# A fused attention, Fourier-mix and FFN kernel: a fourth 8 KB buffer, five FFN tiles resident, other transfer numbers in the list schedule

## The chip, the cores and the metric

The kernel runs on one core of one Trainium2 chip. The metric is device time in microseconds (us), the median of several executions. TensorE is PE, its weight loads PEld, VectorE DVE, ScalarE ACT, GpSimd POOL, and SyncE (SP) issues most of the DMAs.

## The reference, cut to what matters

```python
def reference(q, k, v, w_ch1, w_ch2):        # B=8, H=8, S=576, D=64
    s = where(mask[h], q @ k.T / 8, -1e9)    # window 32; heads 4..7: every 4th of 128
    x = softmax(s) @ v                       # -> x: (8, 576, 512)
    u = x + real(fft(fft(x, axis=1), axis=2))
    un = (u - mean(u)) / sqrt(var(u) + 1e-6) # over the 512 channels
    return u + relu(un @ w_ch1) @ w_ch2      # 512 -> 2048 -> 512
```

The two weights arrive as 64-bit floats; the kernel turns their bits into 32-bit floats itself.

## The kernel before, in words

There are three kinds of work.

**Attention** (lines 475 to 589) runs batch by batch. For a pair of heads it loads `kb`, `tq` and `vt`, multiplies scores (`sc`, line 507), masks and takes the maximum on DVE (`pm`, `mx`, line 515), exponentiates on ACT (line 521), transposes on PE (line 534), multiplies by the values (`av`, line 541), divides on DVE (`xt`, line 553, 96 of these in all) and stores to DRAM (line 588).

**The mix** (`mix`, lines 642 to 818) of a batch loads the stored rows as `x` and `xt` (lines 660 and 669), folds them on POOL and DVE, multiplies by cosine and sine tables (lines 723 and 769), adds on DVE (lines 783 and 785) and POOL, normalises, and stores `us`.

**The FFN** treats the 2048 hidden columns as 16 tiles of 128. A weight tile has a half of `w_ch1` and a half of `w_ch2`. Preparing a half (`prep`, from line 822) takes a 512 KB load (line 842), four DVE instructions (lines 845, 848, 851 and 854), two on ACT (lines 843 and 856) and a POOL subtraction (line 857). Every product is three matmuls, since each operand is held as a high and a low part.

- *Resident tiles*, `NF1` of them (`wa1`, `wa2`, 8 KB a partition for a tile), are prepared at the start, staged through the `ut` buffers. With them the first `NE[c]` tiles of a chunk of 512 tokens are worked off early, while attention and mix still run: `fill` does this for 256 tokens at a time (up: 128x256 matmuls at line 871, `h` at lines 877 and 879; down: line 887) and stores the sums as `part` (lines 907 and 908).
- *Late tiles* take memory that becomes free. When the attention is done, `first()` opens space for `NFA` = 4 tiles (from tile `NF1` on) and a pool with two stage buffers `wst`. When all of the mix and all of the early FFN work is done (but not the stores of its sums), `second()` opens `wbb` for the rest. The DMAs of a half wait for these gates; half one of a tile behind the second gate is staged in `ut`, half two in `wst`.
- The *late stage* goes chunk by chunk, nine chunks. A step is an up of 512 tokens into a bank `ff` (12 matmuls, line 871), relu on ACT and the low part on DVE into a buffer `hh` (lines 877 and 879), and a down (12 matmuls, line 887). `up` of step f+1 stands ahead of `down` of step f. At a chunk's end `finish` adds the parts and stores the output.

The buffers `ut` (`utb`, line 408, `NUT` of them, 8 KB a partition each) serve all of these in turn, in the order in which the program asked for them: staged weight halves, transposed tokens for `fill`, tokens of a late chunk, and the rows in `finish`.

**What sets the order.** Each operation is entered into `Plan` with an engine, a cost, what it reads and writes, and a priority. `Plan.run` (from line 243) is a list scheduler: it goes through its own modelled time, starts on each engine the ready operation of best priority for which a buffer is free, and writes the operations out in that order. Each engine then works strictly in that order. A DMA takes, in that model, its turn in one pipe and then a time to land (lines 317 and 318); SP has at most eight under way.

Of the kernel before, what the change touches and what calls it, by code (L numbers as in the profile page):

```python
# [10 lines left out]
F32R = mybir.dt.float32r  # L11
# [8 lines left out]
P = 128  # L20
KT = C // P
NF = FF // P
NF1 = 6
NE = (6, 6, 6, 6, 5, 5, 4, 4, 0)
TOK = 4 * P
TOK1 = 2 * P
NX = 4
NKB = 3
NV = 4
NTQ = 2  # L30
NUT = 3
NUC = 2
NH = 6
NLATE = 4
# [143 lines left out]
class Plan:  # L178
# [56 lines left out]
    def run(self):  # L235
        ops = self.ops
        busy = {}
        avail, soon = {}, {}
        turn = {t: 0 for t in self.tags}
        events = [0.0]  # L240
        dma = 0.0
        for o in ops:
            busy.setdefault(o.eng, 0.0)
            avail.setdefault(o.eng, [])
            soon.setdefault(o.eng, [])
            if not o.waits:
                heapq.heappush(soon[o.eng], (o.ready, o.num))
                heapq.heappush(events, o.ready)
        order = []
        used, clock = {}, [0, False]  # L250
        lanes = {e: [] for e in busy}

        def place(o, now):
            need = []
            if o.nbytes and len(lanes[o.eng]) >= 8 and lanes[o.eng][-8] > now:
                return False
            for b in o.bufs:
                if b.tag is None or b.ap is not None or b.free_at is not None:
                    continue
                line, k = self.tags[b.tag], turn[b.tag]  # L260
                if line[k] is not b:
                    return False
                if k >= self.slots[b.tag]:
                    old = line[k - self.slots[b.tag]]
                    if old.left or old.free_at > now:
                        return False
                need.append(b)
            for b in need:
                turn[b.tag] += 1
                b.free_at = -1.0  # L270
            return True

        while events:
            now = heapq.heappop(events)
            while events and events[0] <= now:
                heapq.heappop(events)
            again = True
            while again:
                again = False
                for eng in busy:  # L280
                    if busy[eng] > now:
                        continue
                    while soon[eng] and soon[eng][0][0] <= now:
                        _, n = heapq.heappop(soon[eng])
                        heapq.heappush(avail[eng], (ops[n].prio, n))
                    held, got = [], None
                    while avail[eng]:
                        e = heapq.heappop(avail[eng])
                        if place(ops[e[1]], now):
                            got = ops[e[1]]  # L290
                            break
                        held.append(e)
                        if len(held) > 60:
                            break
                    for e in held:
                        heapq.heappush(avail[eng], e)
                    if got is None:
                        continue
                    again = True
                    got.start = now  # L300
                    order.append(got)
                    cost = got.cost
                    if eng == "PE":
                        win = int(now / WINDOW)
                        while clock[0] < win:
                            load = used.get(clock[0], 0.0) / WINDOW
                            clock[1] = load > 0.45 if clock[1] else load > 0.75
                            clock[0] += 1
                        cost *= 1 if clock[1] else 2
                        used[win] = used.get(win, 0.0) + min(cost, (win + 1) * WINDOW - now)  # L310
                        used[win + 1] = used.get(win + 1, 0.0) + max(0.0, now + cost - (win + 1) * WINDOW)
                    end = now + cost
                    busy[eng] = end
                    heapq.heappush(events, end)
                    done = end
                    if got.nbytes:
                        dma = max(dma, end + 0.65) + got.nbytes / 3.6e5
                        done = dma + 1.0
                        lanes[eng].append(done)
                        heapq.heappush(events, done)  # L320
                    for a in got.after:
                        lag = self.OWN[eng] if a.eng == eng else self.LAG[eng]
                        a.ready = max(a.ready, done + lag)
                        a.waits -= 1
                        if not a.waits:
                            heapq.heappush(soon[a.eng], (a.ready, a.num))
                            heapq.heappush(events, a.ready)
                    for b in got.bufs:
                        b.left -= 1
                        b.free_at = max(b.free_at or 0.0, done + self.LAG[eng])  # L330
                        if not b.left:
                            heapq.heappush(events, b.free_at)
        if len(order) != len(ops):
            left = [o for o in ops if o.start is None]
            raise RuntimeError(f"{len(left)} operations can't be placed: {[(o.eng, o.num, o.prio) for o in left[:5]]}")
        self.length = max(busy.values())
        for o in order:
            o.fn()
# [29 lines left out]
def fused_kernel(ctx: ExitStack, tc, q, k, v, w1, w2, seq, tail, chn, alt, mask, ident, perm, flip, out):  # L368
    nc = tc.nc
    plan = Plan()  # L370
# [12 lines left out]
    pools = {}  # L383
# [18 lines left out]
    def ffnb(tag, shape, dtype=F32, bufs=2):  # L402
        return plan.buf(lambda: pools["ffn"], tag, shape, dtype, bufs)

    def fixed(pool_, shape, dtype, name):
        return Buf(ap=pool_.tile(shape, dtype, name=name))

    def utb(i=0):
        return ffnb("ut", [P, 2, KT, TOK1], F32R, NUT)

    flip_sb = fixed(const, [P, 8], I32, "flip_sb")
    wa1 = [fixed(const, [P, 2, KT, P], F32R, f"wa1_{f}") for f in range(NF1)]
    wa2 = [fixed(const, [P, 2, C], F32R, f"wa2_{f}") for f in range(NF1)]
    mask_sb = fixed(heads, [QB, 3, KB], F32, "mask_sb")
# [446 lines left out]
    def prep_w(f, d1, d2, stage, gate, prio):  # L861
        prep(w1.rearrange("(j k) f -> j k f", k=KT)[:, :, P * f:P * f + P], True, d1, stage(0), gate, prio)
        prep(w2[P * f:P * f + P], False, d2, stage(1), gate, prio)
# [148 lines left out]
    def early(c):  # L1012

        return NE[c]

# [19 lines left out]
    n_att = len(plan.ops)  # L1035
    for f in range(NF1):
        prep_w(f, wa1[f], wa2[f], utb, (), P_W + P_WF * f)
# [5 lines left out]
    n_side = len(plan.ops)  # L1043
    split = NF1 + NFA

    def weights(pool_, fs):
        for f in fs:
            wb1[f].ap = pool_.tile([P, 2, KT, P], F32R, name=f"wb1_{f}")
            wb2[f].ap = pool_.tile([P, 2, C], F32R, name=f"wb2_{f}")

    def first():
        att_ctx.close()
        weights(ctx.enter_context(tc.tile_pool(name="wba", bufs=1, side="right")), range(NF1, split))
        pools["stage"] = stage_ctx.enter_context(tc.tile_pool(name="stage", bufs=1, side="right"))
# [10 lines left out]
    def switch(fn, gate, after):  # L1065
        sw = add("NONE", 0.0, fn, (), gate, 0)
        for o in after:
            o.after.append(sw)
            sw.waits += 1

    wb1, wb2 = [[Buf() for f in range(NF)] for i in range(2)]
    gate1, gate2, gate3 = Buf(ap=0), Buf(ap=0), Buf(ap=0)
    switch(first, [gate1] + wb1[NF1:split] + wb2[NF1:split], plan.ops[:n_att])
    switch(second, [gate2] + wb1[split:] + wb2[split:], [o for o in plan.ops[:n_side] if o not in apart])
# [20 lines left out]
    for c in range(NCH):  # L1095
        where, gate = (("wbb", gate2), ("late", gate3))[c % 2]
        ut = load_ut(c, gate, where, LAST + c) if c else ut0
        accs = [bank(t) for t in spare[c % 3]]
        first = early(c)
        for f in range(first, NF):  # L1100
            w = (wb1 if f >= NF1 else wa1)[f]
            h = plan.buf(lambda: pools["wbb"], "hh", [P, 2, TOK], F32R, 3)
            h = up(ut, w, bank("ff"), h, LAST + c + f / NF, cut=True)
            if pend is not None:
                lower(*pend)
            pend = (c, f, h, accs, first, LAST + c + f / NF + 0.1)
# [24 lines left out]
```

## Time and profile before

| | us |
|---|---|
| median of 3 runs | 1156.83 |
| lowest, highest | 1151.93, 1158.43 |
| the profiled execution's own time | 1156.17 |
| its span | 1154.4 |
| PE busy, DVE busy | 1096.1, 595.6 |
| mean granted TensorE clock | 0.985 |

The profiled execution has 1.77 us outside its span and lies 0.66 us below the median. A row of the windows view gives, for a stretch of the span, the busy time of each engine with the number of instructions, the granted clock, the busy share of the DMA engines and their rate. In a row of instruction groups stand line, engine, operation, output <- input, shapes, count, then busy time and the mean duration of one in ns, then the engine's idle time just before and what ended it. Durations of matmuls overlap: the time of one is read from the distance of two starts.

### The profile page before, as it was taken

To read this page: it belongs to the slowest core of one execution; us is meant where nothing else is said; L and a number is where in the kernel's file an instruction comes from. 1 tells how busy PE (TensorE), PEld (TensorE's weight loads), DVE (VectorE), ACT (ScalarE), POOL (GpSimd) and SP (SyncE) were. 2 spreads that over 40 slices of the span, in tenths; PEclk is the share of its full clock that TensorE was granted. 3 is DMA by queue.
4 is the path that set the end of the run, shared out by engine and by line. 5 is a ranking of instruction groups with operands and counts; after the bars stand their busy time and mean duration, and the time that the engine had idled before them with its cause. 6 is when DMAs were issued, how large, how long until landed. Compare 5 with 4: busy or idle time off the path is not lost.

```text
span 1154.4 us, 17385 instructions
## 1 busy us (share of the span) xinstructions
PE 1096.1 (95%) x6112; PEld 920.5 (80%) x6112; DVE 595.6 (52%) x1949; ACT 417.1 (36%) x987; POOL 290.6 (25%) x346
## 2 busy tenths in 40 slices
PE   5878989999999998999998999999999999999998
PEld 4667878887888887889866888888888888888886
DVE  5899887666667657873387414141314141312111
ACT  4876656546455543433243212121212121121210
POOL 1245464233242315540045112020202020020100
PEclk9999999999999999999999999999999999999999
DMA  9985475455374426433354504050505040310201
GB/s 289 261 264 155 130 215 163 143 145 165 103 199 133 126 60 185 132 115 92 83 192 110 146 19 128 19 140 7 146 1 145 2 128 19 104 43 18 74 1 36
DMA packets 100966, 133.71 MB, mean 116 GB/s; under 512 B 9400, under 2 KB 60024, under 8 KB 100880
## 3 DMA queue, kind: packets, MB, share of 16 engines
q1 hardware_dynamic: 97296, 123.71, 37.5%
q0 software_dynamic: 3040, 8.09, 2.6%
q8 instruction: 48, 0.79, 0.3%
q10 hardware_dynamic: 544, 0.82, 0.2%
q14 instruction: 38, 0.31, 0.1%
HBM read 95.82 MB, written 36.75 MB: 115 GB/s over the span
## 4 chain that ended last, share of the span: by engine, by line
PE 73%; DVE 13%; DMA 6%; issue 2%; ACT 2%; POOL 1%; SPq 1%; DVEq 0%; ACTq 0%; POOLq 0%
PE ff L871 27%; PE sc L887 9%; PE mix L887 8%; PE ff L887 6%; PE sc L507 4%; PE pt L887 4%; PE av L887 4%; PE av L541 3%; PE mix L723 2%; PE mix L769 2%; DVE pm L515 2%; DMA x<-xsm 1%; PE pt L534 1%; DMA us<-uc 1%; DMA ut<-in_w_dram 1%
## 5 line engine op out<-in xcount | busy, mean ns | idle before, releaser
L879 DVE SCALAR_TENSOR_TENSOR hh<-ff,hh 128x512 fp32r<-128x512 f32 x102 | 70.1, 688 | 338.5 <-ACT hh L877 329.1
L877 ACT ACTIVATE hh<-ff 128x512 fp32r<-128x512 f32 x102 | 60.8, 596 | 328.5 <-PE ff L871 328.4
L871 PE MATMUL ff<-utwbb,wb 128*128 128x512 f32 x600 | 148.4, 397 | 2.1 <-ACT utwbb L995 1.2
L521 ACT ACTIVATE pm<-pm,mx 96x128 f32<-96x128 f32 x384 | 130.4, 394 | 54.8 <-DVE mx L515 51.8
L871 PEld LDWEIGHTS ff<-utwbb,wb 128*128 128x128 f32 x600 | 113.7, 190 | 29.3 <-POOL utwbb L998 2.5
L871 PE MATMUL ff<-ut,wa 128*128 128x256 f32 x816 | 115.1, 292 | 7.7 <-ACT row L907 4.7
L931 POOL DMA_INDIRECT ut<-us,flip_sb x20 | 19.4, 969 | 385.3 <-DMA out_dram<-ut 291.3
L871 PE MATMUL ff<-utlate,wb 128*128 128x512 f32 x480 | 116.1, 391 | 0.0
L507 PE MATMUL sc<-kb,tq 128*96 128x256 f32 x384 | 107.1, 399 | 8.9 <-DMA kb<-in_k_dram 7.6
L871 PEld LDWEIGHTS ff<-ut,wa 128*128 128x128 f32 x816 | 104.1, 193 | 10.7 <-ACT row L907 5.3
L871 PEld LDWEIGHTS ff<-utlate,wb 128*128 128x128 f32 x480 | 90.1, 188 | 19.8
L541 PEld LDWEIGHTS av<-vt,ptsb 128*96 128x96 f32 x768 | 79.8, 170 | 29.7 <-issue 12.5
L515 DVE CUSTOM_DVE_ANT_0 pm<-sc,mask_sb 96x128 f32<-96x128 f32 x384 | 92.0, 279 | 21.8 <-PE sc L507 17.2
L887 PE MATMUL ff<-wa,h 128*128 128x512 f32 x408 | 101.2, 398 | 0.4 <-DVE h L879 0.4
L541 PE MATMUL av<-vt,ptsb 128*96 128x65 f32 x768 | 84.6, 253 | 16.6 <-DVE xt L553 14.8
L887 PE MATMUL sc<-wb,hh 128*128 128x512 f32 x360 | 93.1, 393 | 5.1 <-DVE hh L879 5.1
L887 PE MATMUL mix<-wb,hh 128*128 128x512 f32 x360 | 92.1, 391 | 0.0
L887 PEld LDWEIGHTS ff<-wa,h 128*128 128x128 f32 x408 | 75.2, 189 | 16.8 <-DVE h L879 0.6
L887 PEld LDWEIGHTS sc<-wb,hh 128*128 128x128 f32 x360 | 67.3, 188 | 21.2 <-DVE hh L879 6.6
L978 DVE STREAM_TRANSPOSE ut<-ut 128x512 f32<-128x512 f32 (+1 forms) x68 | 66.6, 1020 | 31.5 <-DMA ut<-us 29.9
L887 PEld LDWEIGHTS mix<-wb,hh 128*128 128x128 f32 x360 | 67.6, 188 | 14.8
L507 PEld LDWEIGHTS sc<-kb,tq 128*96 128x96 f32 x384 | 56.9, 170 | 22.3 <-DVE kb L450 7.6
(147 smaller groups left out, 1676.2 us busy)
## 6 DMA issues: line engine op xcount, KB each, us to landing
vt<-in_v_dram SPq DMA_DIRECT2D x32, 390.0 KB
us<-uc SPq DMA_DIRECT2D x36, 257.0 KB
tq<-in_q_dram SPq DMA_DIRECT2D x32, 288.0 KB
ut<-in_w_dram SPq DMA_DIRECT2D x18, 512.0 KB
ut<-us SPq DMA_DIRECT2D x36, 256.0 KB
kb<-in_k_dram SPq DMA_DIRECT2D x62, 144.0 KB
part<-row SPq DMA_DIRECT2D x32, 256.0 KB
ut<-part SPq DMA_DIRECT2D x32, 256.0 KB
```

Of the source, the lines that this page charges most:

```text
L507: nc.tensor.matmul(sc()[:QB, 256 * n:256 * n + 256], lhsT=tq()[:, cols], rhs=kb()[:, :, keys], start=True, stop=True,)
L515: nc.vector.tensor_tensor_reduce(pm()[:, i], sc()[:QB, KB * i:KB * i + KB], mask_sb()[:, masks[blocks[i // 2]]], -0.125, 3.0e38, ALU.add, ...
L521: add("ACT", 0.295, lambda i=i: nc.scalar.activation(out=pm()[:, i], in_=pm()[:, i], func=AF.Exp, bias=mx()[:, i:i + 1], scale=-1.0), ((mx ...
L541: add("PE", 0.16, lambda i=i: nc.tensor.matmul(av()[:QB, 65 * i:65 * i + 65], lhsT=pt()[:, i], rhs=vt()[:, i % 2, blocks[i // 2]], start=T ...
L723: nc.tensor.matmul(ps()[:, :NSP], lhsT=lt, rhs=tab, start=(m == 0 and n == 0), stop=(m == 2 and n == count - 1),)
L769: nc.tensor.matmul(ps()[:n, :NEP], lhsT=ys[i]()[:, dt, a, rows], rhs=chn_sb[i]()[:, dt, c], start=(dt == 0 and x == 0), stop=(i == 1 and d ...
L871: nc.tensor.matmul(z()[:, :n_tok], lhsT=wf()[:, a, kk], rhs=ut()[:, p, kk], start=(kk == 0 and n == 0), stop=(kk == KT - 1 and n == 2),)
L877: add("ACT", act(n_tok) - 0.05, lambda: nc.scalar.activation(out=h()[:, 0, :n_tok], in_=z()[:, :n_tok], func=AF.Relu), (z,), ((h, 0),), prio)
L879: add("DVE", dve(n_tok), lambda: nc.vector.scalar_tensor_tensor(h()[:, 1, :n_tok], z()[:, :n_tok], 0.0, h()[:, 0, :n_tok].bitcast(F32), op ...
L887: nc.tensor.matmul(acc(), lhsT=h()[:, a, P * s:P * s + P], rhs=wf()[:, p], start=(first and n == 0), stop=(last and n == 2),)
L931: add("POOL", 1.04, lambda: nc.gpsimd.indirect_dma_start(u(), None, us[idx // 4](), bass.IndirectOffsetOnAxis(ap=flip_sb()[:, 4 * kk + idx ...
L978: nc.vector.transpose(out=o[back], in_=x[:, g])
```

## The change

Four numbers at the top, two in `Plan.run` and one buffer count are changed.

```diff
-NF1 = 6
-NE = (6, 6, 6, 6, 5, 5, 4, 4, 0)
+NF1 = 5
+NE = (5, 5, 5, 5, 5, 5, 5, 5, 0)
...
-NUT = 3
+NUT = 4
...
-                        dma = max(dma, end + 0.65) + got.nbytes / 3.6e5
-                        done = dma + 1.0
+                        dma = max(dma, end + 0.65) + got.nbytes / 3.0e5
+                        done = dma + 2.8
...
-            h = plan.buf(lambda: pools["wbb"], "hh", [P, 2, TOK], F32R, 3)
+            h = plan.buf(lambda: pools["wbb"], "hh", [P, 2, TOK], F32R, 2)
```

Five tiles are prepared at the start and stay resident; the 8 KB of the sixth go to a fourth `ut` buffer. Chunks 0 to 3 have five early tiles in place of six, chunks 6 and 7 five in place of four: 40 early pieces of chunk and tile in place of 42, and 104 late steps in place of 102. The tiles behind the first gate are 5 to 8 (before: 6 to 9), those behind the second 9 to 15, seven in place of six; `hh` has two buffers. In the modelled time a transfer has a pipe of 300 in place of 360 GB/s and lands 2.8 us, not 1.0 us, after it. The schedule is made anew, so instructions move on every engine. Three places follow.

On SP, near the program's start, the loads of the first mix (`x`, `xt`) and what stands just ahead of them; `ut<-in_w_dram` is a weight half. Before:

```order
L492 DMA tq<-in_q_dram 128x576
L490 DMA kb_156<-in_k_dram 64x576 x2
L842 DMA ut<-in_w_dram 128x4x128
L842 DMA ut<-in_w_dram 128x512
L660 DMA x_159<-xsp_59 128x512
L660 DMA x_160<-xsm_67 128x512
L660 DMA x_161<-xsp_59 128x512
```

And now:

```order
L493 DMA vt<-in_v_dram 128x780
L492 DMA tq<-in_q_dram 128x576
L490 DMA kb_156<-in_k_dram 64x576 x2
L660 DMA x_157<-xsp_59 128x512
L660 DMA x_159<-xsp_59 128x512
L660 DMA x_158<-xsm_67 128x512
L660 DMA x_160<-xsm_67 128x512
```

Eight weight halves are issued ahead of the first `x` load before, six now, and the two that stood directly ahead are gone from there.

On SP, the loads of the last mix (`x<-xsp_66`, `x<-xsm_74`) and the first weight halves behind the first gate (`wst<-in_w_dram`). Before:

```order
L616 DMA us_81<-uc 128x514
L842 DMA wst<-in_w_dram 128x4x128
L842 DMA wst<-in_w_dram 128x512
L968 DMA ut<-us_79 32x8x128 x4
L660 DMA x_161<-xsp_66 128x512
L660 DMA x_162<-xsm_74 128x512
```

And now:

```order
L660 DMA x_159<-xsp_66 128x512
L660 DMA x_160<-xsm_74 128x512
L669 DMA xt_161<-xsm_74 1x512
L669 DMA xt_162<-xsm_74 1x512
L616 DMA us_81<-uc 128x514
L908 DMA part_99<-row 128x512
L616 DMA us_81<-uc 128x514
L842 DMA wst<-in_w_dram 128x4x128
L842 DMA wst<-in_w_dram 128x512
```

The weights have moved behind the mix's loads. On DVE, 28 weight instructions stand between the last `xt` (line 553) and the last `sq` (line 785) before, 14 now.

On DVE, in the first chunk of the late stage, the rows around one low part `hh`, with the weight work (`ut`, `wst`) between two of them. Before:

```order
L879 SCALAR_TENSOR_TENSOR hh<-ff,hh 128x512
L854 SCALAR_TENSOR_TENSOR ut<-ut 128x512
L845 TENSOR_SCALAR wst<-wst 128x512
L845 TENSOR_SCALAR ut<-ut 128x512
L848 SCALAR_TENSOR_TENSOR wst<-wst 128x512
L848 SCALAR_TENSOR_TENSOR ut<-ut 128x512
L851 SCALAR_TENSOR_TENSOR wst<-wst 128x512
L978 STREAM_TRANSPOSE ut<-ut 128x4x4x32 x3
L879 SCALAR_TENSOR_TENSOR hh<-ff,hh 128x512
```

And now:

```order
L879 SCALAR_TENSOR_TENSOR hh<-ff,hh 128x512
L854 SCALAR_TENSOR_TENSOR ut<-ut 128x512
L978 STREAM_TRANSPOSE ut<-ut 128x4x4x32 x4
L845 TENSOR_SCALAR wst<-wst 128x512
L848 SCALAR_TENSOR_TENSOR ut<-ut 128x512
L848 SCALAR_TENSOR_TENSOR wst<-wst 128x512
L879 SCALAR_TENSOR_TENSOR hh<-ff,hh 128x512
```

The pattern is the same, but in all 56 weight instructions stand between the low parts of this chunk, where 48 did, and the four transposes stand ahead of one `hh` together. Behind this chunk the order of steps in a chunk is as it was.

## The prediction

> **What bounds the kernel now.** I read the page first, then the windows view cut where the kind of work changes. On the page:
>
> ```profile
> span 1154.4 us, 17385 instructions
> PE 1096.1 (95%) x6112; PEld 920.5 (80%) x6112; DVE 595.6 (52%) x1949; ACT 417.1 (36%) x987; POOL 290.6 (25%) x346
> ...
> DMA  9985475455374426433354504050505040310201
> ```
>
> PE is busy for all but 58 us, so only those 58 us and the granted clock can be won. The cuts come from two groups: the last `xt` ends the attention, the last of line 769 the mix on PE.
>
> ```profile
> L553 DVE TENSOR_TENSOR xt<-av,rinv x96: 387/416/423, 14.3 to 435.4; 96x256 f32<-96x256 f32 x96
> ...
> L769 PE MATMUL mix<-chn,y x288: 277/282/475, 90.6 to 488.0; 128*128 128x258 f32 x96, 128*33 128x258 f32 x48
> ```
>
> The late stage begins at 577.69, after a short wait for its tokens, and in its first chunk PE waits for `hh`:
>
> ```profile
> 577.69 0.73 PE L871 MATMUL ff<-utwbb,wb 128*128 128x512 f32 x2 [1.24 <-ACT utwbb L995]
> ...
> PE sc L887 <- DVE hh L879: 5.1, 3, 3.0
> ```
>
> The stretches (busy PE, PEld, DVE, ACT, POOL, then clock, DMA share, GB/s):
>
> ```profile
> 0.00:54.00 54.00, 38.55 (x240) 28.58 (x240) 38.42 (x222) 34.69 (x97) 11.09 (x18) 0.94 1.00 274
> 54.00:146.00 92.00, 79.10 (x597) 68.44 (x598) 82.13 (x359) 61.53 (x168) 47.53 (x57) 0.96 0.63 189
> 146.00:192.00 46.00, 42.69 (x299) 36.49 (x299) 36.21 (x166) 24.49 (x67) 22.63 (x33) 0.96 0.64 180
> 192.00:440.00 248.00, 241.76 (x1748) 212.92 (x1747) 166.39 (x780) 130.45 (x357) 87.05 (x129) 0.99 0.47 136
> 440.00:488.00 48.00, 42.70 (x257) 37.31 (x257) 40.40 (x76) 21.52 (x46) 25.53 (x28) 0.93 0.58 162
> 488.00:577.70 89.70, 85.80 (x532) 75.78 (x530) 47.63 (x96) 26.73 (x58) 14.47 (x17) 1.00 0.35 100
> 577.70:645.00 67.30, 61.32 (x247) 47.90 (x248) 50.65 (x67) 25.16 (x44) 28.71 (x21) 0.95 0.46 139
> 645.00:1146.00 501.00, 501.00 (x2190) 410.85 (x2189) 130.94 (x183) 92.58 (x153) 53.56 (x47) 1.00 0.24 64
> ```
>
> Four stretches are not PE's. To 54 us transfers are the limit (share 1.00 at 274 GB/s), to 146 us DVE (82.13 of 92). From 440 to 488 DVE again (40.40 of 48), with weights behind the first gate beside the last mix. From 577.7 to 645 PE waits for `hh` behind weight work. From 192 to 440 us and from 645 us on PE is full.
>
> **The change part by part.** *Two early pieces become late steps.* Starts of matmul runs on the chain of waits:
>
> ```profile
> 247.43 5.75 PE ff L871 x48
> 253.17 8.40 PE ff L887 x36
> ...
> 734.58 2.72 PE ff L871 x12
> 740.02 2.72 PE ff L871 x12
> ```
>
> An early piece is 24 narrow ups and 12 downs: 24 x 5.75/48 + 12 x 8.40/36 = 5.68 us. A late step is 740.02 - 734.58 = 5.44 us. Two pieces: **-0.5 us**. PE's total is thus as before. In the new order 93 narrow ups and 48 downs fewer stand ahead of the last matmul of line 769, 93 x 0.120 + 48 x 0.233 = 22.3 us; that stretch shortens, and the late stage takes it back.
>
> *One tile less is prepared at the start.* DVE's groups in the first 140 us, with one mix group further down:
>
> ```profile
> L515 DVE CUSTOM_DVE_ANT_0 pm<-sc,mask_sb 96x128 f32<-96x128 f32 x160 | 38.4, 278 | 9.5 <-PE sc L507 6.5 <-ACT pm L521 1.6 <-PE pt L534 0.8
> L515 DVE DVE_READ_ACCUMULATOR2_ANT mx<- 96x1 f32 x160 | 12.5, 78 | 0.1
> L848 DVE SCALAR_TENSOR_TENSOR ut<-ut 128x512 uint32<-128x512 uint32 x12 | 12.1, 1008 | 0.0
> L851 DVE SCALAR_TENSOR_TENSOR ut<-ut 128x512 uint32<-128x512 uint32 x12 | 10.1, 845 | 0.0
> L854 DVE SCALAR_TENSOR_TENSOR ut<-ut 128x512 f32<-128x512 f32 x12 | 8.9, 745 | 0.0
> ...
> L845 DVE TENSOR_SCALAR ut<-ut 128x512 uint32<-128x512 uint32 x12 | 6.5, 541 | 3.6 <-DMA ut<-in_w_dram 3.6
> ...
> L602 DVE BATCH_NORM_STATS2 stats<-x 128x6 f32<-128x512 f32 x4 | 2.6, 678 | 0.0
> ```
>
> A tile costs DVE 2 x (1.008 + 0.845 + 0.745 + 0.541) = 6.3 us, just where DVE is the limit. By the new order DVE has, at the 36th `xt`, eight weight instructions fewer and four masked pieces (0.278 + 0.078 each) more: -6.3 + 4 x 0.356 = -4.9. At the 48th (about 192 us, where PE becomes the limit) it has eight masked pieces (2.85) and two transposes (2.1, at 1.05, row below) more and one `stats` (0.68) fewer: -6.3 + 2.85 + 2.1 - 0.68 = -2.0. Transfers say much the same: two halves of 524 KB fewer ahead of the first mix's loads at 274 GB/s are 3.8 us, and that mix waits for those:
>
> ```profile
> 60.78 5.56 DMA x<-xsm
> ```
>
> Bounds: 0, if what is pulled ahead fills the gap, and -6.3, with all of it kept. I take **-4.5**, near the row at the 36th `xt`, since transfers and DVE both give.
>
> *The weights move behind the last mix.* Of 40.40 us DVE in 48, 14 weight instructions of 0.78 (6.28/8) go, 11 us. At stake is PE's idle time, 5.3 us, and the clock, (1 - 0.93) x 48 = 3.4 us. Part of the idle time is another wait, which stays:
>
> ```profile
> PE ff L871 <- ACT row L907: 3.1, 1, 3.1
> ```
>
> Bounds: 0 and 8.7 - 3.1 = -5.6. I take half, **-3**. The instructions land in the next stretch, where DVE has 47.63 of 89.7; that covers them.
>
> *A seventh tile behind the second gate.* Load, first weight work, a stall and the last weight work:
>
> ```profile
> 577.65 0.56 SPq L842 DMA_DIRECT2D ut<-in_w_dram  x1
> ...
> 581.98 1.01 DVE L845 TENSOR_SCALAR ut<-ut 128x512 uint32<-128x512 uint32 x1 [10.24 <-DMA ut<-in_w_dram]
> 626.17 1.18 DVE L854 SCALAR_TENSOR_TENSOR wst<-wst 128x512 f32<-128x512 f32 x1
> ...
> L879 DVE SCALAR_TENSOR_TENSOR hh<-ff,hh 128x512 fp32r<-128x512 f32 x10 | 6.8, 680 | 10.6 <-ACT hh L877 10.6
> L978 DVE STREAM_TRANSPOSE ut<-ut 128x512 f32<-128x512 f32 x4 | 4.1, 1052 | 0.0
> ...
> 620.17 1.43 PE L887 MATMUL sc<-wb,hh 128*128 128x512 f32 x5 [3.04 <-DVE hh L879]
> ```
>
> DVE works from 581.98 to 627.35, 45.4 us, on six tiles, four transposes (4.1) and seven `hh` (4.8): 36.5/6 = 6.1 us a tile. With one `hh` a step needs 6.8 us of DVE against 5.44 of PE, so a further tile puts PE 1.3 us further behind. Four tiles lie ready before the gate opens, as before. Bounds: 0, if the slack behind the last tile takes it, and 7 x 1.35 = +9.5, if every tile falls behind. I take **+1.3**, the price of one.
>
> *`hh` with two buffers* costs nothing as long as a step's down ends before the second up behind it:
>
> ```profile
> 1132.86 0.60 ACT L877 ACTIVATE hh<-ff 128x512 fp32r<-128x512 f32 x1 [4.84 <-PE ff L871]
> 1138.30 0.60 ACT L877 ACTIVATE hh<-ff 128x512 fp32r<-128x512 f32 x1 [4.84 <-PE ff L871]
> ...
> 1134.02 1.52 PE L887 MATMUL mix<-wb,hh 128*128 128x512 f32 x6
> ```
>
> ACT fills a buffer at 1138.30 whose reader ended at 1135.54, 2.8 us before; that gap is the cover. Without it a step would pay `hh`'s 0.60 + 0.68 us, over 104 steps 133 us; the order of the steps excludes it.
>
> *The fourth `ut` and the pipe's numbers* cost no instruction; they act through the order that is counted above. A single 512 KB load lands 4.3 us after issue (577.65 to 581.98); the model's 0.5 + 0.65 + 524288/rate + landing gave 3.6 and gives 5.7, and in the crowded start the `x` load of 256 KB took 5.56. The truth lies between the two. [...]
>
> **Sum.** -0.5 - 4.5 - 3 + 1.3 = -6.7 on the profiled execution's 1156.17: 1149.5. The median lies 0.66 above that execution: 1150.2. A measurement of this kernel tells about 0.5% (5.8 us) from no change, so the line is at 1151.05: the forecast stands just beyond it.
>
> **The rivals.** *Nothing moves.* If the pipe was right at 360, the first stretch's order was not at fault, and DVE's room is filled with work that PE only needs later. Then the start keeps only the -2.0 of the 48th `xt`, the last mix gives nothing, and -0.5 - 2.0 + 1.3 leaves 1155.6. For it: from 192 to 440 us PE is full whatever DVE does. Against: DVE's 89% from 54 to 146 us.
>
> *Slower: the second gate.* Half two of the seven tiles goes through two `wst` buffers, and the last such load stands on SP behind loads for `finish` that wait for a `ut` buffer. From the point where DVE's 6.8 us a step meet no finished half, each of the seven steps pays: +9.5, and a stall lowers the clock (five matmuls behind the 3.04 us wait took 1.43 us). With the gains at half, -4, the sum is 1156.8 + 5.5 + 2 for the clock = 1164.3. Against: four tiles of lead.
>
> *A larger gain.* If both stretches give their bounds, -6.3 - 5.6 - 0.5 + 1.3 = -11.1: 1145.7, and with half of the 15.5 us that PE idles to 54 us beside full transfers, 1138. For it: the order now counts on late landings.
>
> **How the numbers follow.** The forecast has 0.45 (its own range 1147 to 1153; 0.35 of it below 1151.05), nothing moves 0.25 (0.02 of it slower), the second gate 0.20, the larger gain 0.10. Faster 0.35 + 0.10 = 0.45; same 0.10 + 0.23 = 0.33; slower 0.20 + 0.02 = 0.22. The range 1140 to 1164 leaves out half of the second gate and a little of the larger gain.
>
> **What would show it.** In the changed profile the last matmul of line 769 should end near 488 - 4.5 - 3 - 22.3 = 458, and the late stage begin near 577.7 - 4.5 - 3 - 11.4 (two early pieces) = 559. DVE's first weight tiles cost 31 us in place of 37.6. Waits of PE for `hh` in the first late chunk near 6.4 us, not 5.1, and none behind it. Wrong: a late stage that begins after 566 (no gain at the start), `hh` waits over 12 us (the second gate), or any wait for `hh` in a later chunk (two buffers too few).

## The result, and the profile after

The changed kernel takes 1128.41 us (six executions, 1127.36 to 1130.22) against 1157.07 of the kernel before (six, 1151.93 to 1158.57). The ratio is 0.976, with a 95% interval of 0.9742 to 0.9778: 28.7 us faster by the medians, where 6.7 were forecast and the range ended at 1140. One of all executions reported here, of `after_3ut` below, was a slow one (1526.79 us at a granted clock of 0.654); it counts in that run's median, which is 1140.15 without it, and not in its ratio. The page of the profile after, in the parts that were shown of before:

```profile
span 1128.1 us, 17317 instructions
PE 1085.5 (96%) x6088; PEld 912.9 (81%) x6088; DVE 589.2 (52%) x1947; ACT 410.6 (36%) x985; POOL 294.9 (26%) x346
...
DMA  9786475656645353522544204050504041411101
```

The span is 26.3 us shorter. PE idles 1128.1 - 1085.5 = 42.6 us where it was 58.3: -15.7. Its busy time fell by 10.6, though its work fell by only 0.5. Nearly all of that is the clock: the mean granted clock went from 0.985 to 0.994, and (1 - clock) x span from 17.3 to 6.8 us.

To see where, both kernels are cut at the same points of the program: the 48th `xt` on DVE, the last (96th) `xt`, the end of the mix on PE, the first late matmul, the first matmul of the second late chunk. The windows view of before (columns as in the prediction):

```profile
0.00:188.50 188.50, 156.84 (x1111) 130.43 (x1112) 153.84 (x728) 118.68 (x325) 78.76 (x103) 0.95 0.74 211
188.50:435.40 246.90, 240.66 (x1732) 211.40 (x1731) 164.87 (x784) 131.32 (x359) 85.88 (x126) 0.99 0.48 138
435.40:488.20 52.80, 47.49 (x298) 42.11 (x297) 45.05 (x91) 22.68 (x49) 29.39 (x34) 0.94 0.56 157
488.20:577.69 89.49, 85.59 (x529) 75.57 (x528) 47.43 (x95) 26.72 (x58) 14.27 (x17) 1.00 0.35 101
577.69:643.48 65.79, 59.80 (x240) 46.65 (x241) 49.13 (x65) 25.16 (x44) 28.71 (x21) 0.95 0.46 140
643.48:1154.40 510.92, 505.67 (x2209) 414.36 (x2207) 135.25 (x190) 92.58 (x153) 53.56 (x47) 1.00 0.24 65
```

And of after:

```profile
0.00:184.30 184.30, 157.83 (x1112) 130.10 (x1113) 149.13 (x728) 117.02 (x325) 76.24 (x100) 0.96 0.73 213
184.30:401.30 217.00, 216.71 (x1605) 192.22 (x1603) 160.89 (x769) 125.20 (x348) 88.95 (x128) 1.00 0.55 156
401.30:443.90 42.60, 41.74 (x283) 37.49 (x283) 33.76 (x75) 17.50 (x41) 23.27 (x31) 1.00 0.55 158
443.90:543.22 99.32, 95.45 (x598) 85.13 (x597) 56.61 (x112) 32.41 (x70) 19.98 (x20) 1.00 0.35 101
543.22:611.76 68.54, 62.60 (x264) 49.13 (x265) 54.47 (x74) 27.93 (x49) 33.61 (x24) 1.00 0.51 157
611.76:1128.10 516.34, 511.18 (x2233) 418.84 (x2231) 134.31 (x191) 90.56 (x154) 52.86 (x46) 1.00 0.23 64
```

Length minus busy PE is idle time. It falls from 31.7 to 26.5 up to the 48th `xt`, from 6.2 to 0.3 in the second stretch, from 5.3 to 0.9 in the third, and stays at 3.9 and near 6 in the next two. The clock column lost something in four of the five stretches ahead of the last, and now in the first alone. The last stretch grew by 5.4 us, one late step. The second and third stretch are 40.1 us shorter in all; 22 of these are work that the new order does later, as the prediction had counted (22.3), and the fourth stretch is 9.8 us longer for it.

The second and third stretch are therefore worth 10.3 us of idle time and some 5 of clock. Of the second the prediction had said that PE is full. PE's waits there, before:

```profile
PE ff L871 <- ACT row L907: 3.1, 1, 3.1
PE av L541 <- DVE xt L553: 2.1, 4, 0.9
PE ff L871 <- DVE h L879: 2.1, 3, 1.2
PE pt L534 <- ACT ptsb L537: 1.8, 1, 1.8
```

And after, from the 48th `xt` to the end of the mix:

```profile
PE mix L745 <- DVE y L729: 0.9, 2, 0.7
PE mix L723 <- DVE ye L751: 0.2, 1, 0.2
```

None of the four of before is left. They were waits for ACT and DVE; for the longest, the chain shown further down has that work in queues behind other instructions. What those engines themselves waited for is the subject of the experiments.

The marks that the prediction had named came earlier than it said: the last matmul of line 769 starts at 443.7 us (458 forecast) and the late stage begins at 543.22 (559 forecast). None of its three signs of being wrong came: the late stage doesn't begin after 566, the waits for `hh` in the first late chunk are 4.9 us, and no later chunk waits for `hh`. All three watched for a smaller gain.

### The profile page after: what moved, and what is told of

The parts are those of the page before. It is cut to its first block, busy times and chain, and to the rows that moved or that the text cites. A ratio compares the mean times of both kernels' runs of the same rounds, so it can differ in the third digit from the quotient of the medians.

```text
span 1128.1 us, 17317 instructions
## 1 busy us (share of the span) xinstructions
PE 1085.5 (96%) x6088; PEld 912.9 (81%) x6088; DVE 589.2 (52%) x1947; ACT 410.6 (36%) x985; POOL 294.9 (26%) x346
## 4 chain that ended last, share of the span: by engine, by line
PE 81%; DVE 11%; DMA 3%; issue 2%; POOL 1%; ACT 1%; SPq 0%; ACTq 0%; DVEq 0%
PE ff L871 30%; PE sc L887 10%; PE mix L887 9%; PE ff L887 5%; PE sc L507 5%; PE av L541 5%; PE pt L887 4%; PE av L887 4%; PE mix L769 3%; PE pt L534 2%; PE mix L723 2%; PE pt L871 2%; DVE ut L978 1%; PE av L871 1%; DMA ut<-in_w_dram 1%
## 5 line engine op out<-in xcount | busy, mean ns | idle before, releaser
L871 PE MATMUL ff<-utwbb,wb 128*128 128x512 f32 x660 | 160.7, 392 | 2.5 <-ACT utwbb L995 1.4
L871 PEld LDWEIGHTS ff<-utwbb,wb 128*128 128x128 f32 x660 | 123.6, 188 | 31.4 <-POOL utwbb L998 2.3
L871 PE MATMUL ff<-utlate,wb 128*128 128x512 f32 x528 | 127.4, 391 | 0.0
L507 PE MATMUL sc<-kb,tq 128*96 128x256 f32 x384 | 107.0, 398 | 10.5 <-DMA kb<-in_k_dram 8.3
L871 PEld LDWEIGHTS ff<-utlate,wb 128*128 128x128 f32 x528 | 99.1, 188 | 21.8
L887 PE MATMUL sc<-wb,hh 128*128 128x512 f32 x396 | 102.5, 393 | 4.9 <-DVE hh L879 4.9
L871 PE MATMUL ff<-ut,wa 128*128 128x256 f32 x720 | 102.5, 290 | 2.4 <-DVE h L879 2.4
L887 PE MATMUL mix<-wb,hh 128*128 128x512 f32 x396 | 101.3, 391 | 0.0
L871 PEld LDWEIGHTS ff<-ut,wa 128*128 128x128 f32 x720 | 91.7, 189 | 4.4 <-DVE h L879 3.0
L887 PE MATMUL ff<-wa,h 128*128 128x512 f32 x360 | 88.2, 396 | 0.0
L887 PEld LDWEIGHTS ff<-wa,h 128*128 128x128 f32 x360 | 66.0, 188 | 14.3
L978 DVE STREAM_TRANSPOSE ut<-ut 128x512 f32<-128x512 f32 (+1 forms) x68 | 65.8, 1017 | 12.0 <-DMA ut<-us 11.9
```

What stands on the lines that cost most here:

```text
L507: nc.tensor.matmul(sc()[:QB, 256 * n:256 * n + 256], lhsT=tq()[:, cols], rhs=kb()[:, :, keys], start=True, stop=True,)
L871: nc.tensor.matmul(z()[:, :n_tok], lhsT=wf()[:, a, kk], rhs=ut()[:, p, kk], start=(kk == 0 and n == 0), stop=(kk == KT - 1 and n == 2),)
L887: nc.tensor.matmul(acc(), lhsT=h()[:, a, P * s:P * s + P], rhs=wf()[:, p], start=(first and n == 0), stop=(last and n == 2),)
L978: nc.vector.transpose(out=o[back], in_=x[:, g])
```

## The experiments

At first three theories stood against each other. **A**: the fourth `ut` buffer lets tokens for the early FFN work stand ready. **B**: the transfer numbers do it; an order counted on later landings puts fewer instructions at the head of a queue while their transfer is still under way. **C**: the scheduler's order is a draw (a matter of chance), and any change of a number deals another. **D**, less filler and moved weight work, joined them. Ratios are to the kernel before on the same chip; that kernel's median lay between 1156.8 and 1159.6 us in the five sets of runs.

**The parts apart.** Four kernels: the two transfer numbers alone on the kernel before; the changed kernel with the old transfer numbers; the changed kernel with three `ut` buffers; five tiles alone on the kernel before.

```diff
 # dma_alone, from before
-... + got.nbytes / 3.6e5     -done = dma + 1.0
+... + got.nbytes / 3.0e5     +done = dma + 2.8
 # room_alone, from after
-... + got.nbytes / 3.0e5     -done = dma + 2.8
+... + got.nbytes / 3.6e5     +done = dma + 1.0
 # after_3ut, from after
-NUT = 4
+NUT = 3
 # tiles_alone, from before
-NF1 = 6, NE = (6, 6, 6, 6, 5, 5, 4, 4, 0)
+NF1 = 5, NE = (5, 5, 5, 5, 5, 5, 5, 5, 0)
```

> Before with the two transfer numbers alone (300 GB/s, landing 2.8 us); six tiles, three ut buffers. Theory A (the fourth ut buffer lets tokens for the early FFN work stand ready, so PE has filler at each wait): 1150 to 1160, PE idle between the 48th and the 96th xt stays near 6 us. Theory B (an order counted on late landings keeps the engines' queues from stopping at a transfer): 1130 to 1142, that idle time under 2 us. Theory C (any new order differs by chance): no use in either sign, 1140 to 1165.

Measured: 1145.02 us, ratio 0.9883 (0.9844 to 0.9922).

> After with the old transfer numbers (360 GB/s, landing 1.0 us): five tiles, four ut buffers, two hh. Theory A: 1128 to 1136, PE idle between the 48th and the 96th xt under 1 us. Theory B: 1145 to 1156, that idle time near 6 us. Theory C: anything from 1125 to 1160.

Measured: 1162.2 us, ratio 1.0032 (1.0004 to 1.006).

> After with three ut buffers. Theory A: 1144 to 1156, the idle time between the 48th and the 96th xt is back. Theory B: 1128 to 1136. The 5 us that one tile less gives at the start stay in both.

Measured: 1140.54 us, ratio 0.9843 (0.9793 to 0.9894).

> Before with five resident tiles and five early tiles a chunk alone (three ut, three hh, old transfer numbers). Theories A and B: the start gives about 5 us and no more, 1148 to 1154. A third theory, D (less filler and 14 weight instructions moved behind the last mix are the gain): 1130 to 1140.

Measured: 1158.49 us, ratio 0.9993 (0.9969 to 1.0017).

A falls as the whole cause: with the old numbers the fourth buffer gives nothing. Of D, less filler gives nothing by itself; the other half was hardly tried, since 24 of the 28 weight instructions still stand ahead of the last `sq` in `tiles_alone`. B holds for about half: the numbers give 1.2% with the old tiles. The sizes were missed by every theory: `dma_alone` lies 3 us above B's range, `room_alone` above all of them, `after_3ut` between A and B, `tiles_alone` 4.5 us above A and B. The idle time from the 48th to the 96th `xt` tells more. First `room_alone`, then `after_3ut`:

```profile
187.74:418.51 230.77, 222.78 (x1619) 193.92 (x1618) 163.83 (x769) 127.25 (x351) 86.50 (x124) 1.00 0.52 147
```

```profile
184.04:406.14 222.10, 220.01 (x1627) 194.33 (x1626) 161.03 (x771) 125.33 (x350) 91.14 (x132) 1.00 0.55 153
```

With the fourth buffer and the old numbers it is 8.0 us; with the new numbers and three buffers it is 2.1. It goes with the numbers, as B had it. The same cuts for `dma_alone`, up to the second late chunk:

```profile
0.00:197.30 197.30, 165.86 (x1118) 136.46 (x1119) 155.16 (x746) 121.13 (x334) 75.11 (x99) 0.93 0.71 205
197.30:434.60 237.30, 234.98 (x1730) 209.08 (x1728) 165.00 (x766) 126.18 (x350) 88.67 (x130) 1.00 0.49 140
434.60:478.40 43.80, 41.29 (x272) 36.51 (x271) 36.78 (x76) 18.42 (x41) 23.05 (x31) 1.00 0.57 155
478.40:571.73 93.33, 87.96 (x553) 78.08 (x552) 56.12 (x110) 30.79 (x66) 19.70 (x20) 1.00 0.42 113
571.73:633.95 62.22, 58.24 (x240) 46.05 (x241) 49.02 (x65) 25.39 (x44) 28.08 (x21) 0.97 0.51 148
```

And for `tiles_alone`:

```profile
0.00:182.80 182.80, 154.15 (x1088) 127.79 (x1089) 146.55 (x717) 115.87 (x320) 73.47 (x99) 0.94 0.74 212
182.80:414.60 231.80, 224.79 (x1630) 197.02 (x1628) 163.19 (x779) 128.62 (x353) 87.55 (x129) 0.99 0.52 146
414.60:464.50 49.90, 44.32 (x297) 39.27 (x296) 43.39 (x86) 21.45 (x48) 28.06 (x33) 1.00 0.53 156
...
564.43:639.49 75.06, 66.67 (x265) 52.00 (x265) 55.92 (x74) 28.59 (x49) 31.10 (x23) 0.93 0.47 137
```

With the numbers alone the idle time of the second and third stretch is 2.3 and 2.5 us; with the tiles alone it is 7.0 and 5.6, no better than before. The tiles do bring the 48th `xt` forward, from 188.5 to 182.8. But PE has 2.7 us less work ahead of that mark, and idles only 3.0 us less (28.7). The first late chunk then takes 75.06 us, 9.3 more than before for one more step of 5.4, and the gain of the start is given back.

**Rate, landing, and which transfers.** All on the changed kernel's tiles and buffers.

```diff
 # land_room:  / 3.6e5, landing 2.8      rate_room:  / 3.0e5, landing 1.0
 # tok_late:   / 3.6e5, landing 2.8 for the token loads (line 968), 1.0 for all others
 # tok_early:  / 3.0e5, landing 1.0 for the token loads, 2.8 for all others
 # mixpath_late: / 3.6e5, landing 2.8 for lines 588, 660 and 669, 1.0 for all others
+                        done = dma + (2.8 if got.land else 1.0)
```

> After's tiles and buffers, landing 2.8 us, pipe as before at 360 GB/s. Theory B1 (landing alone is the gain): 1126 to 1134, DVE's waits of transposes (line 978) for token loads near 12 us. Theory B3 (the pipe's rate is the gain): 1150 to 1162. Half and half: near 1145.

Measured: 1142.13 us, ratio 0.9887 (0.9864 to 0.991).

> After's tiles and buffers, pipe 300 GB/s, landing as before at 1.0 us. Theory B1: 1152 to 1162, those waits of DVE above 25 us. Theory B3: 1126 to 1136.

Measured: 1149.18 us, ratio 0.9943 (0.9917 to 0.9969).

> After's tiles and buffers with the old transfer numbers, except that the token loads (line 968) land after 2.8 us in the model. Theory B1t (the gain is the transposes of tokens, which no longer stand at the head of DVE's queue while their load is under way): 1130 to 1140, DVE's waits of line 978 for loads down from 41 us to under 15. Theory B2 (every late landing counts, the x and weight loads as much): 1148 to 1158.

Measured: 1157.72 us, ratio 0.9998 (0.9974 to 1.0022).

> After, except that the token loads land after 1.0 us in the model. Theory B1t: 1145 to 1155, DVE's waits of line 978 back above 25 us. Theory B2: 1130 to 1138.

Measured: 1137.85 us, ratio 0.9837 (0.9814 to 0.986).

> After's tiles and buffers with the old transfer numbers, except that the stores of xt (line 588) and the loads of x and xt (lines 660 and 669) land after 2.8 us in the model. Theory B1x (the landing matters through the mix's round trip through DRAM, store then load): 1140 to 1148, as with every landing late (1142), POOL's waits of line 672 for x down from 49 us to under 30. Theory B2 (it is spread over all transfers, or over none in particular): 1152 to 1160.

Measured: 1158.25 us, ratio 0.9991 (0.9972 to 1.001).

B1t falls: late token loads alone leave the time of the kernel before, and with the token loads alone early DVE's waits for them are back (39.5 us over the whole span, 10.2 of them up to 620 us, against 11.9 in the changed kernel), while the time stays near that of the two neighbours tried below (1137). B1x falls in the same way, though its own wait did fall as that theory had it: POOL's wait of line 672 for `x`, up to 620 us, in `room_alone` and in `mixpath_late`:

```profile
POOL t L672 <- DMA x<-xsm: 49.3, 11, 7.0
```

```profile
POOL t L672 <- DMA x<-xsm: 22.2, 5, 7.3
```

So neither wait as such is what costs. From 1162.2 us landing gives 20 and rate 13, both 34 (17, 10 and 31 by the ratios, as the sets of runs differ): both count. What is left is B2, the landing of all transfers together, or that of transfers which no run set apart: the weight loads, the loads of q, k and v, and the stores of `us` and `part`.

**How much is the draw.** The landing is set a little off 2.8, with each of the three sets of tiles and buffers, and a little off 1.0 on the kernel before.

```diff
 # land_25, land_31, land_4: after with landing 2.5, 3.1, 4.0
 # ut3_25, ut3_31:           after_3ut with landing 2.5, 3.1
 # old_25, old_31:           dma_alone with landing 2.5, 3.1
 # before_08, before_12:     before with landing 0.8, 1.2
```

> After with landing 2.5 us in place of 2.8. Theory B (landing and rate near what the chip does give a good order): 1126 to 1134. Theory C (a draw by chance): anything from 1125 to 1150, as likely as not above 1136.

Measured: 1136.84 us, ratio 0.9806 (0.9778 to 0.9835).

> After with landing 3.1 us. Theory B: 1126 to 1134. Theory C: anything from 1125 to 1150, as likely as not above 1136.

Measured: 1137.03 us, ratio 0.981 (0.9779 to 0.984).

> After with landing 4.0 us, beyond nearly every landing of the trace. Theory B: a little slower than after, 1130 to 1140, since work waits in the order for transfers that have long landed. Theory C: as at 3.1.

Measured: 1144.94 us, ratio 0.9882 (0.9853 to 0.9911).

> After with three ut buffers and landing 2.5 us. If the fourth buffer is worth something, this and the run at 3.1 with three buffers lie above the four-buffer kernels at the same landings (1136.8 and 1137.0), near 1140 to 1148. If the 12 us between after and after_3ut were the draw, they lie at 1132 to 1138.

Measured: 1140.36 us, ratio 0.9854 (0.9806 to 0.9902).

> After with three ut buffers and landing 3.1 us: as for landing 2.5. Buffer of worth: 1140 to 1148; draw alone: 1132 to 1138.

Measured: 1139.86 us, ratio 0.9834 (0.9797 to 0.987).

> Before's tiles and buffers (six tiles, three ut), pipe 300 GB/s, landing 2.5 us. If the transfer numbers alone are worth about 13 us whatever the draw: 1140 to 1149. If 1145 at 2.8 was a lucky draw: 1150 to 1158.

Measured: 1142.74 us, ratio 0.9853 (0.9814 to 0.9893).

> Before's tiles and buffers, pipe 300 GB/s, landing 3.1 us: as for landing 2.5. 1140 to 1149, or 1150 to 1158 if the 1145 at 2.8 was lucky.

Measured: 1149.17 us, ratio 0.9914 (0.9885 to 0.9944).

> Before with landing 0.8 us in place of 1.0. If before is an ordinary draw of its kind: 1152 to 1164. If it was unlucky: under 1150.

Measured: 1166.02 us, ratio 1.006 (1.0038 to 1.0082).

> Before with landing 1.2 us in place of 1.0. If before is an ordinary draw of its kind: 1150 to 1160. If it was unlucky: under 1148.

Measured: 1158.84 us, ratio 1.0003 (0.9981 to 1.0026).

| ratio to before | landing 2.5 | 2.8 | 3.1 | mean |
|---|---|---|---|---|
| old tiles, three `ut`, 300 GB/s | 0.9853 | 0.9883 | 0.9914 | 0.988 |
| five tiles, three `ut` | 0.9854 | 0.9843 | 0.9834 | 0.984 |
| five tiles, four `ut` | 0.9806 | 0.976 | 0.981 | 0.979 |

By these means the transfer numbers give 1.2% (14 us), the moved tile 0.4% (5 us), the fourth buffer 0.5% (6 us), and the order that the change happened to get another 0.3% below the mean of its row (4 us; against its two neighbours alone it is 0.5%). The middle two steps are no larger than the spread of the draws and the intervals, so their sign is likely, their size is not settled. The steps are counted in this order; the tile and the buffer give nothing with the old numbers (`tiles_alone`, `room_alone`). The step of the tile also has the third `hh` buffer less. The kernel before was no unlucky draw: its two neighbours are as slow or slower. Landing at 4.0 loses 8 us to 2.5 and 3.1, so later is not always better (of the 15 transfers on before's chain of waits 11 took under 6.0 us, which is what 4.0 gives for 256 KB); its granted clock is 0.85 up to 57.59 us and 0.77 from there to 102.00, which is some 19 us of lost clock, where the changed kernel has some 3 up to the same point (89.24).

C is thus part of the answer: the two neighbours of the changed kernel lie at 1137 us, above B's 1126 to 1134. It isn't the whole. In all 20 kernels, cut at the same points, the idle time of PE in the second and third stretch together is 1.2 to 7.0 us in the twelve in whose model all transfers, or all but the token loads, land after 2.5 us or more (`land_room` at 360 GB/s: 6.2), and 10.4 to 16.4 us in the eight others (`rate_room` at 300 GB/s: 10.4). No kernel of one group reaches into the other. Ahead of the 48th `xt` the two groups don't differ so: 26.5 to 31.4 us and 28.1 to 32.6.

## Why the prediction was wrong

**The step that failed** is the sentence that the fourth `ut` and the pipe's numbers "cost no instruction; they act through the order that is counted above". Only three places had been counted, and a change of the transfer numbers deals the whole order anew. The numbers alone are worth 14 us, twice the whole forecast. In `dma_alone` PE idles 3.9 us less than before in the second stretch, 2.8 less in the third and 2.0 less in the first late chunk; the start gains nothing (31.4 against 31.7, at a clock of 0.93) and the fourth stretch loses 1.5. In the changed kernel idle time and lost clock together fell by about 7 us in the first stretch, 8 in the second, 8 in the third and 3 in the first late chunk; the forecast had 4.5, nothing, 3, and a loss of 1.3.

**"From 192 to 440 us ... PE is full"** was a misreading of rows that stood in the prediction. 248 us against 241.76 busy are 6.2 us of idle time, and a clock of 0.99 is 2 more. Nearly all of this went (0.3 us of idle time is left, at a clock of 1.00). A share of 97% looks like a bound; in microseconds it was as large as the whole forecast.

**The weights behind the last mix** were right in kind and too small: -3 was taken, with -5.6 as the bound. Idle time fell by 4.4 and the clock's loss by about 3.4 (before had 6.8 us at 0.50, shown in the last section): -7.8. The bound was wrong because a wait of 3.1 us for `row` was said to stay. In the changed kernel it is gone; in the chain of before it stood behind the same weights. On ACT:

```profile
456.24 0.62 ACT L995 CAST ut<-ut 128x512 fp32r<-128x512 f32 x1 [2.57 <-DVE ut L978]
456.76 0.58 ACT L907 COPY row<-ff 128x512 f32<-128x512 f32 x1
```

on DVE:

```profile
452.33 0.69 DVE L854 SCALAR_TENSOR_TENSOR wst<-wst 128x512 f32<-128x512 f32 x1
452.93 0.68 DVE L848 SCALAR_TENSOR_TENSOR wst<-wst 128x512 uint32<-128x512 uint32 x1
454.15 2.06 DVE L978 STREAM_TRANSPOSE ut<-ut 128x512 f32<-128x512 f32 x2 [0.54 <-DMA ut<-us]
```

and on PE:

```profile
457.39 2.75 PE L871 MATMUL ff<-ut,wa 128*128 128x256 f32 x12 [3.12 <-ACT row L907]
```

The copy `row` that frees a PE bank stands on ACT behind a cast, the cast waits for transposes, and those stood on DVE behind weight work and then waited 0.54 us for their load. In these rows the wait passes on: the transposes start at 454.15, the cast at 456.24, the copy at 456.76 and PE at 457.39, after 3.12 us under another name. Which edit moves the weights the prediction didn't say. It is mostly the transfer numbers: between the last `xt` and the last `sq` the order has 28 weight instructions before, 24 with the tiles alone, 17 with the transfer numbers alone, and 14 after.

**One tile less at the start**, -4.5, was right in kind: the 48th `xt` came 4.2 us earlier. That this is so near the forecast is partly luck, since the mark moves with the order: it comes at 182.8 with the tiles alone and at 197.3 with the numbers alone, against 188.5, and in the changed kernel idle time and lost clock ahead of it fell by 7. DVE's weight work up to 140 us fell from 37.6 to 29.6 us (31 forecast). With the old numbers the gain was lost again further on: the rival that nothing moves had that time nearly right (1155.6; `tiles_alone` 1158.49).

**The seventh tile**, +1.3, came out lower in the changed kernel. The first late chunk grew by 2.75 us with a step of 5.44 more, so it lost 2.7 less. PE's waits for `hh` there were 4.9 us in place of the forecast 6.4:

```profile
580.99 1.43 PE L887 MATMUL sc<-wb,hh 128*128 128x512 f32 x5 [1.36 <-DVE hh L879]
588.14 1.45 PE L887 MATMUL sc<-wb,hh 128*128 128x512 f32 x5 [1.40 <-DVE hh L879]
595.50 1.45 PE L887 MATMUL sc<-wb,hh 128*128 128x512 f32 x5 [1.58 <-DVE hh L879]
```

These are three of four short waits; before had three, one of 3.04, and a clock of 0.95, where it now stays at 1.00. The rival of the second gate shows in part with the old numbers: `tiles_alone` lost 9.3 - 5.4 = 3.9 us there, where that rival had 9.5.

**Two `hh` buffers** cost nothing, as forecast: PE is busy for all of 620 to 1120 us, and ACT still waits for its up ahead of nearly every `hh` there, most often 4.84 or 4.93 us.

**The pipe.** The rival that nothing moves had the wider pipe as its condition; no run shows 360 GB/s to be the chip's rate. The runs decide for the narrower: 300 in place of 360 alone took 10 to 13 us from `room_alone`. That does not measure the pipe; it shows only which number in the schedule serves this kernel. The rate at full share, 274 GB/s in the first 54 us of before, had pointed there.

What stays open is how the transfer numbers save 14 us instruction by instruction. The sum of what DVE, ACT and POOL wait for transfers up to 620 us went from 90 us to 65 with the numbers alone and to 75 with the whole change, while in `land_4` it is 42 at 1145 us; so that sum alone doesn't set the time. Neither of the two paths that were set apart, the tokens and the mix, carried it; the others weren't tried.

## What to carry to other kernels

Where a list scheduler writes the order, its model of a transfer is part of the kernel: try its rate and landing like any other number, and expect a change of them to count on every engine, not where loads are dense alone. Whether the trace's own figure is the best one is not shown: the single load of 4.3 us in before would be a landing of 1.4 at 300 GB/s (4.3 - 0.5 - 0.65 - 1.75), and no run had that. Before an edit of such a kernel is believed, run two neighbours of it that differ in a number of no meaning; here such steps move the time by up to 0.6%, 7 us. And read stretches in microseconds of idle time and lost clock, not in shares.

## What the runs showed of the hardware

A stall was seen to cost more than its length. In before the wait of 3.12 us that ends at 457.39 is followed by 6.8 us at a granted clock of 0.50, 3.4 us of lost clock, with one more wait of 1.20 us in it:

```profile
457.60:464.40 6.80, 5.60 (x26) 5.31 (x26) 5.88 (x9) 2.91 (x8) 4.63 (x6) 0.50 0.63 196
464.40:471.00 6.60, 6.60 (x45) 6.09 (x45) 6.11 (x10) 3.80 (x10) 3.55 (x4) 1.00 0.30 61
```

In those 6.8 us 26 matmuls ran, in the next 6.6 us 45, some of them wider. Behind the wait of 3.04 us that ends at 620.17 the clock was 0.50 from 622 to 624 us: three `pt` matmuls of line 887 took 1.45 us from 621.43 on, and three from 628.50 on 0.84. The five that the prediction names for this took their 1.43 us ahead of that, at a clock of 1.00. A shorter wait was followed by a lower clock too: in before, behind one of 1.80 us at 279, it was 0.52 for 3.4 us, while after the three waits of 1.36 to 1.58 us in the changed kernel's first late chunk the clock stays at 1.00.

```profile
279.21 0.47 PE L534 MATMUL pt<-perm_sb,pm 96*128 96x96 f32 x3 [1.80 <-ACT ptsb L537]
```

```profile
280.30:283.70 3.40, 3.40 (x17) 2.97 (x15) 2.61 (x18) 2.17 (x7) 2.45 (x4) 0.52 0.51 146
```

Of the 26.3 us that the span lost, 10.5 are lost clock, though no edit touched it; no run here set the clock apart from the waits.
